# Moving the input and the first forward transform of a spectral layer ahead of a kernel's set-up

## The chip, the cores and the metric

The kernel runs on one core of one Trainium2 chip. The metric is the device time of one execution in microseconds (us); the median over runs is what counts. A core has five engines that run side by side, each through its own queue in order: PE (TensorE, matrix products), DVE (VectorE), ACT (ScalarE), POOL (GpSimd) and SP (SyncE, which here only issues DMA transfers). An instruction that waits holds up everything behind it on its engine.

## The reference

Four layers are interleaved on one sequence `x` of 2048 rows and 512 columns: A, B, A, B, each as `x = x + layer(layernorm(x))`, in 32-bit floats.

```python
def A(x, w_r, w_i):                       # spectral layer
    X = rfft2(x, axes=(-2, -1))           # 2048 x 512 -> 2048 x 257 complex
    return irfft2(X * (w_r + 1j * w_i), s=(2048, 512), axes=(-2, -1))

def B(u, A_re, A_im, B_re, B_im, C_re, C_im, log_dt, Dskip):   # state space layer
    dt = exp(log_dt)[:, None]                                  # 512 channels, 128 states
    P = exp((dt * (A_re + 1j*A_im))[:, :, None] * arange(2048))
    K = einsum("dn,dnl,dn->dl", C, P, dt * B).real             # 512 kernels of 2048 taps
    return causal_convolution(u, K) + u * Dskip                # by FFTs of length 4096
```

The layer norm takes mean and variance over the 512 columns. Layer B's kernel `K` depends on the weights alone, is computed once, and serves both B layers.

## The kernel before

All transforms are matrix products with tables of cosines and sines. `x` lies in SBUF as 128 partitions by 16 slices by 512; a *slice* is one of the 16 values of the index `s2`.

The first part of the program, up to about 370 us, does three things that don't depend on each other.

**The set-up of B's kernel (`setup_k`, L969).** From the weights (`kN`, `kLn`, loaded to `an` and `ld`) DVE and ACT work out the factors of the exponents: phases in turns (`th`, and three more quarters of a tile `F`) and logarithms. `parts` (L957) splits each factor in three bfloat16 parts: a cast on ACT, a subtraction on DVE, a store to DRAM (`spe`, `spt`), three times over. `load_k` (L1026) reads them back, 16 rows at a time, in another layout. All loads of `load_k` wait for all stores.

**The units of B's kernel.** 32 units in eight batches of four. A batch begins with six exponentials (`exp_k`, L1043 to L1059: two products on PE, one ACT exponential of 128x1024 each, at L1057). A unit (`unit_k`, L1061) then rounds its phase (ACT L1071, DVE L1073 and L1074), takes a cosine and a sine (ACT L1076 and L1077), multiplies (DVE L1084 and L1085, POOL L1088 and L1089), makes 64 small products on PE (L1101) and copies the result (DVE L1112). ACT has to load another function table between exponentials, sines and square roots (ACT_TABLE_LOAD in the profile). Pieces called `turn_k` (copies at L1150) and `spectra_k` (copies at L823) carry finished kernels on.

**Layer A, first pass.** `loads` (L467) brings the weights `kN` and then `x` in eight transfers of two slices. `moments` (L488) takes mean and variance of a slice on DVE; `spread` (L497) turns four slices' variances into 1/sqrt. `forward_a` (L533) is the forward transform of one slice: the norm (here on DVE, L518), sum and difference of the halves on POOL (L543, L544), two more sums with reversed operands on DVE (L549, L550) and a copy of two columns on ACT (L551), four products on PE (L556, L559), a copy out of PSUM on ACT (L564). When all 16 are there, 16 pieces `first_a` (L652) do the transform over the slices, the product with the weights and the way back: `fold_d` on PE (L577), copies on ACT (L667, L668), products (L677 to L681), DVE L686 to L688 and L694, POOL L692, products (L703 to L711), a copy on ACT (L715). `inv_a` (L718) goes back to `x`.

The second part (layer B, A, B) starts when both are done.

**What sets the order.** The program is written out piece by piece by a planner (`Clock`, L197). It holds a set of Python generators, each with a rank; at each step it takes, of the pieces that its own estimate of times (`COST`, L40) says can start by about the same moment, the one with the lowest rank, and lets it emit its instructions up to the next `yield`. What a `yield` names are the engine, the buffers and the events waited for; a leading `+` says that the piece need not wait for what it has just emitted. So the order on every engine is fixed when the kernel is built. In `plan_k` the set-up has rank -99 (L1161); in `plan_a` the moments have -20 and the forwards `RANK[0] + RANK[1] * s2`, that is -4 and up (L1223, L1227).

Buffers come from rings: a table gives a name, a size and how many there are (`RINGW`: the temporaries `a`, `b`, `c`, `d` of a forward). The five buffers `G` for the tables of `first_a` lie in the space of `x` itself (`RINGX`), so their loads wait for the norms that read that part of `x`.

## Time and profile before

| what | value |
|---|---|
| median of 3 runs | 863.92 us (862.75 to 873.96) |
| the profiled execution | 864.92 us, of which the span from first to last instruction is 863.1 us |
| PE busy | 661.6 us, 77% of the span |
| DVE busy | 537.3 us, 62% |
| ACT busy | 406.4 us, 47% |
| POOL busy | 290.6 us, 34% |
| mean granted clock of PE | 0.934 |

Line numbers such as L1057 are those of the kernel before; the changed kernel has other numbers for the same lines. A row of the timeline gives the start and the duration in us, the engine, the line, the operation, the tile written, the tile read, their shape, and in square brackets the idle time ahead of it with what ended it. An answer by windows gives for each stretch the length and, for each engine, busy time and number of instructions, then the granted clock of PE, the share of the DMA engines and GB/s. DVE and POOL instructions overlap their neighbours by some 0.1 us, so what one costs in a row of them is the distance from start to start.

### The profile page before, as it was taken

The numbers are of one execution on the slowest core, as the hardware profiler recorded it, in microseconds if no ns is written. First come the engines' busy times: TensorE is split into PE (matmuls) and PEld (weight loads), VectorE is DVE, ScalarE is ACT, GpSimd is POOL, SyncE is SP. The second block draws the span as 40 slices with busy tenths as digits, with TensorE's granted clock in tenths as the row PEclk, the third lists the DMA queues.
The fourth block names the chain that finished last, engine by engine and source line by source line (L and its number), as shares of the span: only waits on it lengthen the run. The fifth ranks groups of instructions, "written<-read, shape, count | busy, mean of one in ns | idle before, by whom it ended". The sixth has DMA issues, their size and how long they took to land. (4 is left out here: it accounts for less than half of the span.)

```text
span 863.1 us, 23197 instructions
## 1 busy us (share of the span) xinstructions
PE 661.6 (77%) x9828; PEld 418.7 (49%) x9828; DVE 537.3 (62%) x1054; ACT 406.4 (47%) x742; POOL 290.6 (34%) x259
## 2 busy tenths in 40 slices
PE   0048677978999799797885876889877999488876
PEld 0036454646657444356332642767665544234555
DVE  6988866557848685963441643686876666267512
ACT  1447677487778857744243132175441234323120
POOL 0037745336526431500422314174443000067310
PEclk9999789899999999999898888899997999889988
DMA  9134005332524754469969971901641145957857
GB/s 330 46 124 125 13 13 160 107 116 90 178 91 149 259 163 135 155 213 242 249 156 262 272 275 42 221 2 37 225 170 43 26 123 142 276 148 188 233 128 211
DMA packets 86630, 132.48 MB, mean 153 GB/s; under 512 B 5660, under 2 KB 58144, under 8 KB 85888
## 3 DMA queue, kind: packets, MB, share of 16 engines
q1 hardware_dynamic: 54400, 101.65, 39.6%
q10 hardware_dynamic: 32128, 29.37, 11.8%
q8 instruction: 77, 1.26, 0.6%
q14 instruction: 25, 0.20, 0.1%
HBM read 70.31 MB, written 27.13 MB: 113 GB/s over the span
## 5 line engine op out<-in xcount | busy, mean ns | idle before, releaser
L880 POOL TENSOR_TENSOR wk<-wk 128x512 f32<-128x512 f32 x64 | 80.1, 1275 | 246.8 <-DVE wk L874 162.2
L874 DVE TENSOR_TENSOR wk<-ps,Y 128x512 f32<-128x512 f32 x128 | 79.1, 683 | 77.1 <-issue 28.2
L1088 POOL TENSOR_TENSOR Y<-wk,Y 128x1024 f32<-128x1024 f32 x32 | 76.4, 2386 | 111.7 <-issue 63.1
L915 PE MATMUL ps<-wk,cRbT 64*128 64x256 f32 x512 | 74.1, 438 | 21.7 <-DMA wk<-Ya 14.8
L556 PE MATMUL ps<-cRa,wk 128*128 128x256 f32 x128 | 36.0, 406 | 57.1 <-POOL wk L543 57.1
L915 PEld LDWEIGHTS ps<-wk,cRbT 64*128 64x128 f32 x512 | 61.3, 219 | 35.0 <-issue 15.7
L891 PE MATMUL ps<-wk,Y 32*32 32x256 f32 x2048 | 58.9, 405 | 19.3 <-POOL wk L880 10.7
L921 DVE TENSOR_TENSOR x<-x,ps 128x256 f32<-128x256 f32 x64 | 24.8, 408 | 72.6 <-PE ps L915 72.5
L770 PE MATMUL ps<-wk,cRb 128*32 128x256 f32 x1024 | 61.3, 381 | 6.4 <-DVE wk L518 4.0
L772 ACT COPY wk<-ps 128x512 f32<-128x512 f32 x64 | 37.1, 587 | 57.6 <-PE ps L770 35.6
L1073 DVE SCALAR_TENSOR_TENSOR wk<-wk,ps 128x1024 f32<-128x1024 f32 x32 | 38.9, 1214 | 40.2 <-ACT wk L1071 40.2
L732 PE MATMUL ps<-cDaT,apart 128*32 128x256 f32 x256 | 60.3, 385 | 1.3 <-DVE x L747 1.1
L543 POOL TENSOR_TENSOR wk<-wk 128x256 f32<-128x256 f32 x32 | 25.6, 800 | 90.1 <-DVE wk L518 55.5
L556 PEld LDWEIGHTS ps<-cRa,wk 128*128 128x128 f32 x128 | 23.4, 202 | 61.1 <-POOL wk L543 57.9
L770 PEld LDWEIGHTS ps<-wk,cRb 128*32 128x32 f32 x1024 | 37.8, 110 | 31.1 <-DVE wk L518 5.0
L1041 PE MATMUL ps<-wk,Y 96*128 96x512 bf16 x128 | 41.2, 401 | 13.0 <-DVE Y L1084 6.0
L1101 PE MATMUL ps<-Y 128*32 128x64 f32 x2048 | 40.0, 236 | 14.2 <-POOL Y L1089 7.4
L891 PEld LDWEIGHTS ps<-wk,Y 32*32 32x32 f32 x2048 | 27.1, 105 | 48.9 <-POOL wk L880 23.2
L899 ACT COPY Ya<-ps 128x256 f32<-128x256 f32 x64 | 19.4, 385 | 63.9 <-PE ps L891 46.1
L1057 ACT ACTIVATE Y<-ps 128x1024 f32<-128x1024 f32 x48 | 46.5, 1034 | 6.1 <-PE ps L1041 6.0
L518 DVE TENSOR_SCALAR wk<-x,mv,rs 128x256 f32<-128x256 f32 (+1 forms) x80 | 35.3, 481 | 21.6 <-PE ps L770 15.5
L1101 PEld LDWEIGHTS ps<-Y 128*32 128x32 f32 x2048 | 34.4, 120 | 29.1 <-issue 15.2
(190 smaller groups left out, 1542.9 us busy)
## 6 DMA issues: line engine op xcount, KB each, us to landing
Y<-khat SPq DMA_DIRECT2D x24, 512.0 KB, 7.9
yk<-wk ACTq DMA_DIRECT2D x32, 256.0 KB, 2.6
wk<-Y SPq DMA_DIRECT2D x16, 512.0 KB, 4.6
wk<-Ya SPq DMA_DIRECT2D x16, 512.0 KB, 4.6
Y<-in_W_dram SPq DMA_DIRECT2D x12, 515.0 KB, 4.0
x<-in_cPa_dram SPq DMA_DIRECT2D x16, 384.0 KB, 3.2
Y<-in_cGa_dram SPq DMA_DIRECT2D x12, 384.0 KB
x<-in_W_dram SPq DMA_DIRECT2D x16, 258.0 KB, 3.5
```

Source lines behind the costliest of these rows:

```text
L556: nc.tensor.matmul(p[:, 0:256], pq[:, i, :], self.Ra[:, i:i + 2].rearrange("p a m -> p (a m)"), start=i == 0, stop=i == 1)
L732: nc.tensor.matmul(p[32 * i:32 * i + 32, o:o + 256], self.folded(r, i)[:, b, s2].rearrange("p g m -> p (g m)"), self.DaT[:, b, :], start=b ...
L770: self.nc.tensor.matmul(p[o:o + 32, 256 * h:256 * h + 256], self.Rb[:, 2 * h + j, 32 * a:32 * a + 32], xn[s], start=True, stop=True)
L874: nc.vector.tensor_tensor(t[c][:, j], x, kh[:, j, ::-1, :] if c else kh[:, j], op=OP.mult)
L880: nc.gpsimd.tensor_tensor(Z[:, :, c], t[0][:, :, c], t[1][:, :, c], op=op)
L891: nc.tensor.matmul(v[j][h][i:i + 32], gi[o:o + 32, j, 4 + 2 * s + c, :], Z[o:o + 32, j, c, :], start=c == 0, stop=c == 1)
L915: nc.tensor.matmul(q[s], self.RbT[o, i, :], y[o, i, :], start=i == 0, stop=i == 3)
L1041: self.nc.tensor.matmul(p, f[:, c:c + 128], self.oh[:k, o:o + 512], start=True, stop=True)
L1057: nc.scalar.activation(m[:, :, 1024:] if i == 2 else m[:, i, :1024], p.rearrange("p (i m) -> p i m", i=2) if i == 2 else p, AF.Exp)
L1073: nc.vector.scalar_tensor_tensor(s, c, MAGIC, p, op0=OP.subtract, op1=OP.subtract)
L1088: nc.gpsimd.tensor_tensor(E[:, 0, :1024], c, m[:, :1024], op=OP.mult)
L1101: nc.tensor.matmul(pk[32 * j:32 * j + 32, 64 * e:64 * e + 64], E1[:, r, i, :], E2[:, r, i], start=r == 0, stop=r == 1)
```

## The change

Five edits, all in the first part of the program, but for small changes of shape in the second forward pass.

- `loads`: `x`'s first transfer, then layer A's table `cRa`, then `x`'s second transfer stand ahead of the weights `kN`; the remaining transfers of `x` follow.
- Ranks: the moments have -120, the forwards -116 and up, and of the set-up one chain has -130 and the others -110 and -105. So the forwards are emitted among the set-up.
- `NORMS[0]` is True: the norms of the first forwards are one ACT instruction (`Identity` with scale and bias), with one more small DVE instruction for each four slices (the bias).
- In the first pass (`r == 0`) the two reversed sums on DVE and the small copy on ACT are gone. POOL makes the difference in two instructions, the second with both operands reversed, and PE makes the four sums by adding two products in PSUM; one of them uses the negated table. A forward has then six products in place of four. A row of the table `cDa` is placed elsewhere to match.
- `setup_k` is split: `setup_b` (the complex product, logarithms, arctangent), `setup_a` (phases, `th`), and four `setup_f` that cast and store a quarter of `F` each. They share DVE and ACT instruction by instruction. The casts have three buffers for `hi` and `hj` and write quarters: 15 casts and 15 stores in place of 6 and 6.

```diff
-NORMS = False, False, True, False
+NORMS = True, False, True, False
...
     def loads(self):
         src = self.io["A_x"].rearrange("b (p s) d -> p (b s) d", p=128)
-        self.load_n()
-        self.mark("kN")
-        yield self.emitted("kN")
         for q in range(8):
-            if q == 0:
-                self.load_ra()
             self.nc.sync.dma_start(self.x[:, 2 * q:2 * q + 2, :], src[:, 2 * q:2 * q + 2, :])
-            for i, f in ((0, "load_h"), (5, "load_da"), (7, "load_rb")):
+            self.mark("in", q)
+            yield self.emitted(("in", q))
+            for i, f in ((0, "load_ra"), (1, "load_n"), (5, "load_da"), (6, "load_h"), (7, "load_rb")):
                 if i == q:
                     getattr(self, f)()
-            self.mark("in", q)
-            yield self.emitted(("in", q))
+            if q == 1:
+                self.mark("kN")
+                yield self.emitted("kN")
...
     def forward_a(self, r, s2, st):
-        yield "DVE a", self.after((id(st), s2 // 4)), ...
+        yield ("DVE a" if r else "ACT a"), self.after((id(st), s2 // 4)), ...
         xn = self.norm(s2, st)
         yield "POOL c d"
...
-        nc.gpsimd.tensor_tensor(uv.rearrange("p a b -> p (a b)"), lo, hi, op=OP.subtract)
+        if r:
+            nc.gpsimd.tensor_tensor(uv, lo, hi, op=OP.subtract)
+        else:
+            nc.gpsimd.tensor_tensor(uv[:, 0:129], lo[:, 0:129], hi[:, 0:129], op=OP.subtract)
+            nc.gpsimd.tensor_tensor(uv[:, 130:258], lo[:, 255:127:-1], hi[:, 255:127:-1], op=OP.subtract)
...
-        for b in range(2):
-            nc.tensor.matmul(p[:, 256 + 128 * b:384 + 128 * b], F[:, b, :], self.Ra[:, 0], start=True, stop=True)
+        if r:
+            for b in range(2):
+                nc.tensor.matmul(p[:, 256 + 128 * b:384 + 128 * b], F[:, b], R, start=True, stop=True)
+        else:
+            for i, o in enumerate((p[:, 256:384], p[:, 384:512])):
+                nc.tensor.matmul(o, uv[:, i:i + 128], R, start=True, stop=False)
+                nc.tensor.matmul(o, uv[:, 129 + i:257 + i], R if i else nR, start=False, stop=True)
...
-    def parts(self, a, shape, tag, out):
+    def parts(self, a, j, out):
         for p in range(3):
-            yield "ACT " + tag
-            hi = self.w(tag, shape).bitcast(BF)[:, :int(np.prod(shape[1:])) * 2]
-            nc.scalar.copy(hi, a)
-            if p < 2:
-                nc.vector.tensor_tensor(a, a, hi, op=OP.subtract)
-            nc.sync.dma_start(out(p), hi)
+            yield "ACT"
+            nc.scalar.copy(j[p], a)
+            nc.sync.dma_start(out(p), j[p])
+            self.mark("factors")
+            if p < 2:
+                yield "DVE"
+                nc.vector.tensor_tensor(a, a, j[p], op=OP.subtract)
...
+    def setup_f(self, a, r):
+        yield "ACT", self.after(("F", a), 1)
+        yield from self.parts(self.F[:, a, r], [h[:, a, r] for h in self.hi], ...)
...
-        yield -99, self.setup_k()
+        yield -130, self.setup_b()
+        yield -110, self.setup_a()
+        for a in range(2):
+            for r in range(2):
+                yield -105, self.setup_f(a, r)
...
-            yield -20, moments(s2)
+            yield -120, moments(s2)
...
-            yield RANK[0] + RANK[1] * s2, self.forward_a(0, s2, st)
+            yield -116 + s2, self.forward_a(0, s2, st)
```

Three places show what this does to the order. First DVE at the very start. `Y` holds the set-up's temporaries, `x` the input, `mv`, `rs`, `nb` the moments. Before:

```order
L1193 MEMSET quarter 128x1
L981 TENSOR_TENSOR Y<-Y 128x512 x2
L982 TENSOR_SCALAR Y<-Y 128x512
L953 TENSOR_SCALAR Y<-Y 128x512
L954 TENSOR_SCALAR Y<-Y 128x512
L955 SCALAR_TENSOR_TENSOR Y<-Y 128x512
```

Now, behind the moments of the first three slices:

```order
L491 BN_STATS st<-x 128x6
L492 BN_AGGR mv<-st 128x2
L501 RECIPROCAL rs<-rs 128x4
L504 SCALAR_TENSOR_TENSOR nb<-mv,rs 128x4
L1021 TENSOR_TENSOR Y<-Y 128x1024
L1023 TENSOR_TENSOR Y<-Y 128x1024
L1025 TENSOR_TENSOR Y<-Y 128x512
L1026 TENSOR_TENSOR Y<-Y 128x512
```

Four slices' moments and their 1/sqrt stand ahead of the set-up, which now begins with its other chain.

Second, ACT around the first batch of exponentials (L1057 before, L1102 now; `Ya` takes the forwards' copies, L564 before). Before:

```order
L551 COPY wk<-wk 128x2
L1057 ACT_TABLE_LOAD
L1057 ACTIVATE Y<-ps 128x1024
L551 COPY wk<-wk 128x2
L564 COPY Ya<-ps 128x128x4
L1057 ACTIVATE Y<-ps 128x1024
L564 COPY Ya<-ps 128x128x4
L551 COPY wk<-wk 128x2
L1057 ACTIVATE Y<-ps 128x2x512
L1057 ACTIVATE Y<-ps 128x1024
```

Now (`apart` takes the result of a `first_a`, L676 and L677 are its first copies, L971 is the set-up's last cast):

```order
L676 COPY wk<-ps 128x64
L677 COPY wk<-ps 128x448
L971 CAST Y<-Y 128x512
L724 COPY apart<-ps 128x64x8 x2
L1102 ACT_TABLE_LOAD
L1102 ACTIVATE Y<-ps 128x1024 x2
L1102 ACTIVATE Y<-ps 128x2x512
L1102 ACTIVATE Y<-ps 128x1024 x2
L1102 ACTIVATE Y<-ps 128x2x512
L1116 ACTIVATE wk<-ps,magic 128x1024 x2
```

The exponentials had 13 of the 16 forwards beside and behind them; now they have none, and two `first_a` are done and two more begun ahead of them.

Third, DVE at the end of the set-up (L965 before and L976 now are the subtractions between casts). Before:

```order
L965 TENSOR_TENSOR Y<-Y 128x2048
L503 RECIPROCAL rs<-rs 128x4
L493 BN_STATS st<-x 128x6
L494 BN_AGGR mv<-st 128x2
L493 BN_STATS st<-x 128x6
L494 BN_AGGR mv<-st 128x2
L493 BN_STATS st<-x 128x6
L494 BN_AGGR mv<-st 128x2
L518 TENSOR_SCALAR wk<-x,mv,rs 128x512 x2
```

Now:

```order
L1066 SCALAR_TENSOR_TENSOR Y<-Y 128x512
L1068 TENSOR_TENSOR Y<-Y 128x512
L976 TENSOR_TENSOR Y<-Y 128x512 x7
L695 TENSOR_TENSOR x<-ps,x 128x514
L696 TENSOR_TENSOR x<-ps,x 128x257
L697 TENSOR_TENSOR x<-ps,x 128x257
L976 TENSOR_TENSOR Y<-Y 128x512
L703 TENSOR_TENSOR x<-x 128x257
L695 TENSOR_TENSOR x<-ps,x 128x514
```

The moments and norms that followed the set-up are gone from there, and the set-up's last two subtractions stand behind the first products of `first_a` (L695 to L697).

Further down the first part's order on ACT differs in how many pieces of `first_a` and `turn_k` lie between two batches of exponentials. From the eighth batch on, ACT has the same instructions in the same order as before, to the end of the program, but for the small copy of the second forward pass.

More of the change, by code (lines that the diff above doesn't have):

```diff
@@ L535, in forward_a @@
         nc = self.nc
-        yield "DVE a", self.after((id(st), s2 // 4)), self.emitted(("grouped", 0, 1), 8 * r)
+        yield ("DVE a" if r else "ACT a"), self.after((id(st), s2 // 4)), self.emitted(("grouped", 0, 1), 8 * r)
         xn = self.norm(s2, st)
@@ new lines, in setup_a @@
+        self.turns_of(F[:, 1, 0], th, 32, k)
+        v.scalar_tensor_tensor(F[:, 1, 0], th, -0.5, F[:, 1, 0], op0=OP.mult, op1=OP.add)
+        self.mark("th")
+        yield "ACT hj hj hj"
+        hj = [self.w("hj", [128, 256]).bitcast(BF) for p in range(3)]
+        yield from self.parts(th, hj, lambda p: self.spt[p])
+    def setup_f(self, a, r):
+        yield "ACT", self.after(("F", a), 1)
+        yield from self.parts(self.F[:, a, r], [h[:, a, r] for h in self.hi], lambda p: self.spe[p, a, :, 512 * r:512 * r + 512])
@@ L987, in setup_k, with setup_b @@
+    def setup_b(self):
+        nc = self.nc
+        v = nc.vector
+        yield "DVE", self.after("kN")
+        an, F = self.an, self.F
+        four = [128, 4, 128]
+        an4 = an.rearrange("p r (c n) -> p r c n", c=4)
         ta, tb, w, u = (self.w(t, [128, 2, 512]) for t in ("W", "W", "U", "U"))
+        g, k2 = (self.w("k", [128, 512]) for _ in range(2))
         two = [128, 2, 512]
         v.tensor_tensor(ta, an[:, 4:6], an[:, 2:3].to_broadcast(two), op=OP.mult)
+        yield "+DVE"
@@ L990, in setup_k @@
         v.tensor_tensor(tb, an[:, 4:6], an[:, 3:4].to_broadcast(two), op=OP.mult)
+        yield "+DVE"
         v.tensor_tensor(w[:, 0], ta[:, 0], tb[:, 1], op=OP.subtract)
         v.tensor_tensor(w[:, 1], ta[:, 1], tb[:, 0], op=OP.add)
+        yield "ACT"
         nc.scalar.activation(u, w, AF.Abs)
-        g, k2 = (self.w("k", [128, 512]) for _ in range(2))
-        ln = an[:, 0:2]
+        ln = an[:, 2:4]
+        yield "DVE"
         v.scalar_tensor_tensor(ln[:, 0], u[:, 0], 1e-37, u[:, 1], op0=OP.max, op1=OP.max)
-        v.reciprocal(g, ln[:, 0])
+        for h in range(2):
+            yield "+DVE"
+            o = slice(256 * h, 256 * h + 256)
+            v.reciprocal(g[:, o], ln[:, 0, o])
@@ L1006, in setup_k @@
         v.tensor_tensor(k2, k2, u[:, 0], op=OP.add)
+        for h in range(2):
+            yield "+DVE"
+            o = slice(256 * h, 256 * h + 256)
+            v.reciprocal(k2[:, o], k2[:, o])
+        yield "+DVE"
         v.tensor_tensor(tb[:, 0], w[:, 1], g, op=OP.mult)
-        v.reciprocal(k2, k2)
         v.tensor_tensor(tb[:, 0], tb[:, 0], k2, op=OP.mult)
+        yield "ACT"
         nc.scalar.activation(tb[:, 0], tb[:, 0], AF.Arctan)
+        yield "+DVE"
         v.scalar_tensor_tensor(ln[:, 0], ln[:, 1], 0.5, ln[:, 0], op0=OP.mult, op1=OP.add)
-        v.tensor_tensor(F[:, 1, 1].rearrange("p (c n) -> p c n", c=4), an4[:, 0],
+        v.tensor_tensor(F[:, 1, 1].rearrange("p (c n) -> p c n", c=4), ln[:, 0].rearrange("p (c n) -> p c n", c=4),
@@ L1020, in setup_k @@
         v.tensor_tensor(f, f, tb[:, 0], op=OP.add)
-        yield "DVE"
-        yield from self.parts(th, [128, 256], "hj", lambda p: self.spt[p])
-        yield from self.parts(F.rearrange("p a r m -> p (a r m)"), [128, 1024], "hi", lambda p: self.spe[p].rearrange("a d m -> d a m"))
-        self.mark("factors")
+        self.mark("F", 1)
     def load_k(self, b):
-        yield "SP sq st", self.after("factors")
+        yield "SP sq st", self.after("factors", 15)
         sq, self.st[b] = self.w("sq", [96, 512]), self.w("st", [48, 512], BF)
```

72 lines of the change are left out of this document (43 added, 29 removed).

## The prediction

> **What bounds the kernel now.** The chain that ended last reaches back to 639 us only, so I begin with the busy time by windows, in the first 80 us.
>
> ```profile
> 0.00:20.00 20.00, 0.00 (x0) 0.00 (x0) 13.39 (x20) 3.05 (x5) 0.20 (x4) 1.00 0.91 324
> 20.00:40.00 20.00, 0.00 (x0) 0.00 (x0) 17.57 (x31) 9.93 (x11) 0.00 (x0) 1.00 0.19 68
> 40.00:60.00 20.00, 4.25 (x14) 3.59 (x15) 17.31 (x36) 7.87 (x10) 4.47 (x6) 1.00 0.27 97
> 60.00:80.00 20.00, 19.16 (x103) 14.43 (x103) 15.32 (x31) 15.42 (x30) 16.43 (x22) 1.00 0.63 182
> ```
>
> DVE has the set-up almost alone; PE and POOL do nothing for 55 us, then everybody is busy. The timeline gives the set-up's beginning, its last subtraction, its last cast, the read that waits for the last store, and the first exponentials' table load; the last row is from the tile `spe`:
>
> ```profile
> 5.32 1.29 DVE L981 TENSOR_TENSOR Y<-Y 128x512 f32<-128x512 f32 x2 [4.37 <-DMA Y<-in_kN_dram]
> 49.47 2.29 DVE L965 TENSOR_TENSOR Y<-Y 128x2048 f32<-128x2048 f32 x1 [0.77 <-ACT Y L963]
> 52.31 1.90 ACT L963 CAST Y<-Y 128x2048 bf16<-128x2048 f32 x1 [2.68 <-DMA spe<-Y]
> 57.03 0.93 SPq L1032 DMA_DIRECT2D Y<-spe  x1
> 63.10 1.28 ACT L1057 ACT_TABLE_LOAD   x1
> DMA to landing us min/median/max: 2.9/2.9/2.9
> ```
>
> From the end of the last cast (54.2) to the table load are 8.9 us: a store that lands after 2.9, a read, two products, and ACT copies of forwards that stand ahead. Each of the eight batches begins with this load. They stand at the edges of these windows (the eighth at 322.77):
>
> ```profile
> 63.10:104.52 41.42, 31.68 (x268) 23.15 (x267) 34.15 (x53) 28.90 (x47) 30.94 (x31) 0.91 0.28 82
> 104.52:131.71 27.19, 20.99 (x326) 13.81 (x324) 19.34 (x30) 22.66 (x27) 14.48 (x9) 0.83 0.05 12
> 131.71:178.30 46.59, 39.24 (x501) 27.32 (x502) 30.29 (x48) 28.49 (x38) 20.38 (x15) 0.93 0.47 149
> 178.30:207.97 29.67, 22.25 (x315) 14.40 (x317) 20.51 (x29) 23.80 (x28) 15.49 (x10) 0.94 0.26 81
> 207.97:244.52 36.55, 33.50 (x479) 23.88 (x468) 26.53 (x42) 26.80 (x35) 16.77 (x13) 1.00 0.50 155
> 244.52:279.70 35.18, 33.59 (x445) 22.84 (x444) 23.88 (x40) 27.81 (x36) 16.87 (x13) 0.95 0.37 115
> 279.70:322.77 43.07, 35.95 (x572) 17.63 (x571) 32.59 (x57) 29.98 (x37) 17.80 (x11) 0.96 0.62 208
> ```
>
> No engine is full. The short batches are near ACT's work (22.7 of 27.2, 23.8 of 29.7), the long ones near PE's (33.5 of 36.6). So a batch costs its own ACT time and something for each piece of layer A beside it. From the eighth load on the instructions stand in the same order on all engines before and after. The whole change is therefore two numbers: how much later the first table load stands, and how much shorter the way from the first load to the eighth is.
>
> **The way from the first load to the eighth.** ACT's work in the first part, by line:
>
> ```profile
> L1057 ACT ACTIVATE Y<-ps 128x1024 f32<-128x1024 f32 x48 | 46.5, 1034 | 6.1 <-PE ps L1041 6.0
> L1076 ACT ACTIVATE wk<-wk,quarter 128x1024 f32<-128x1024 f32 x32 | 36.7, 1147 | 14.8 <-DVE wk L1074 14.0 <-ACT wk L1150 0.6
> L1071 ACT ACTIVATE wk<-ps,magic 128x1024 f32<-128x1024 f32 x32 | 35.7, 1127 | 15.2 <-PE ps L1041 11.0 <-POOL Y L1089 2.9 <-ACT wk L1150 1.3
> L1077 ACT ACTIVATE ps<-wk 128x1024 f32<-128x1024 f32 x32 | 32.3, 1011 | 0.0
> L1150 ACT COPY wk<-ps 128x512 f32<-128x512 f32 x24 | 14.1, 589 | 8.7 <-DMA khat<-wk 3.1 <-PE ps L1145 2.8 <-DMA yk<-wk 1.5
> ```
>
> A batch alone is 6 x 1.03 + 4 x (1.15 + 1.13 + 1.01) + 2 table loads of 1.28 = 21.9 us. By the order, windows two to six hold 15 pieces of `first_a` (I count its first and second half as a half each) and 18 copies of `turn_k` and `spectra_k`, which I price at 0.59 each (L1150). These windows last 175.2 us in sum, so a `first_a` costs (175.2 - 5 x 21.9 - 18 x 0.59) / 15 = 3.7 us. The first window holds half a `first_a` and 13 forwards: (41.4 - 21.9 - 1.8) / 13 = 1.36 us for a forward. That is about what POOL takes for one (from start to start 1.46, below).
>
> After the change the same windows hold no forward, 12.5 instead of 15.5 `first_a`, and the same copies; the seventh is unchanged. Saved by these prices: 13 x 1.36 + 3 x 3.7 = 28.7 us.
>
> The windows aren't straight in their pieces, though: the one with four `first_a` (46.6) is 6.4 above this line, those with two are 1 to 2 below it (27.2 against 29.3). The change also spreads the pieces: 3, 2, 1.5, 1.5, 1.5 and 3 to a window. Priced by their nearest windows (27.2 for two, 29.7 with copies, 35.2 for the last, 31.5 halfway for the first) the six last 27.2 + 28.5 + 30.5 + 28.5 + 35 + 31.5 = 181 in place of 216.6: 35 us. I take **31**, nearer to the line, since one window makes the difference and I can't tell its excess from its clock of 0.93. The lower end: if `first_a` only fills time in which ACT idles, 17.7 remain; the upper is 35.
>
> **How much later the first load stands.** The rows I step with: moments, a two-input sum, an immediate scaling and a reciprocal of 512 columns on DVE; norms on ACT; PE's four products of a forward; POOL's first sum of two forwards in a row, between which lies the second.
>
> ```profile
> 43.22 0.66 DVE L493 BATCH_NORM_STATS2 st<-x 128x6 f32<-128x512 f32 x1
> 44.02 0.66 DVE L493 BATCH_NORM_STATS2 st<-x 128x6 f32<-128x512 f32 x1
> 13.17 0.68 DVE L992 TENSOR_TENSOR Y<-Y 128x512 f32<-128x512 f32 x1
> 22.16 0.43 DVE L1001 TENSOR_SCALAR Y<-Y 128x512 f32<-128x512 f32 x1
> 15.70 3.35 DVE L997 RECIPROCAL Y<-Y 128x512 f32<-128x512 f32 x1
> 551.66 1.50 ACT L516 ACTIVATE wk<-x,nb,rs 128x512 f32<-128x512 f32 x2
> 63.50 1.03 PE L556 MATMUL ps<-cRa,wk 128*128 128x256 f32 x4
> 64.36 0.61 PE L559 MATMUL ps<-cRa,wk 128*128 128x128 f32 x4
> 64.81 1.03 PE L556 MATMUL ps<-cRa,wk 128*128 128x256 f32 x4
> 577.43 0.77 POOL L543 TENSOR_TENSOR wk<-wk 128x256 f32<-128x256 f32 x1
> 578.89 0.77 POOL L543 TENSOR_TENSOR wk<-wk 128x256 f32<-128x256 f32 x1
> ```
>
> A forward on PE goes from 1.31 to 1.76 us (0.86 + 2 x 0.45). On POOL the halved difference costs 0.45 an instruction (an estimate: half of the 0.73 from start to start, and 0.1 for what is fixed), 1.6 a forward; no row has POOL read backwards. DVE reads backwards in L549 and pays nothing for it, so I take nothing; the bounds are 0 and double price (0.9 x 16 = 14 us, of which POOL's idle time covers about half).
>
> What decides is how DVE and POOL get along:
>
> ```profile
> 56.34 0.72 POOL L543 TENSOR_TENSOR wk<-wk 128x256 f32<-128x256 f32 x1
> 56.42 0.80 DVE L549 TENSOR_TENSOR wk<-wk 128x127 f32<-128x127 f32 x1 [1.21 <-POOL wk L544]
> 58.33 0.28 DVE L549 TENSOR_TENSOR wk<-wk 128x127 f32<-128x127 f32 x1
> 64.58 0.54 DVE L518 TENSOR_SCALAR wk<-x,mv,rs 128x512 f32<-128x512 f32 x1
> 64.66 1.04 POOL L543 TENSOR_TENSOR wk<-wk 128x256 f32<-128x256 f32 x1 [0.52 <-DVE wk L550]
> ```
>
> A sum of 0.28 us takes 0.80 when POOL is inside one: it ends 0.16 after POOL does. The other way round POOL takes 1.04 in place of 0.72. So they run in turn, each saving some 0.1 us of overlap. The Trainium skill has this as a rule (SBUF — State Buffer, section "SBUF: two separate sides"): DVE instructions with two SBUF inputs or in a two-port mode and GpSimd instructions take one port pair as an exclusive lock. It speaks against this change, which puts 16 forwards of POOL beside a set-up of just such DVE instructions; the rows agree. Without it the sum is that of the first rival.
>
> Now the steps, with times in the new kernel.
>
> To 17 us: before, the set-up began at 5.3 with the first half of `kN`; now `x`'s first transfer lands about there, the moments of four slices take 4 x 0.8, and after the square root the first norm starts near 9. `kN` lands near 10, behind 1 MB more. The product of `setup_b`, 2 x 1.15 + 2 x 0.61, and the first forwards take turns until 15; two moments to 17.
>
> To 33: Abs waits on ACT behind the copies of two forwards, whose products PE makes slowly after a long rest, until 19.6. Then DVE does 0.7 + 3.35 + 1.2 + 2 x 0.8 + 0.6 + 0.45 = 7.9, to 27.5, and ACT three table loads, Ln, Exp and the second group's square root: 3 x 1.28 + 1.06 + 0.63 + 0.2 = 5.7. The fifth norm starts at **33**. POOL has been idle for 14 us: the order on ACT puts the set-up's logarithm ahead of it.
>
> To 58: up to the last square root ACT has 6 norms, 4 copies, the arctangent and two table loads, 4.5 + 2 + 0.6 + 2.6 = 9.7, and waits some 4 for POOL and PE: 47, with five forwards done on POOL. DVE stands still from 43 on, as its queue waits for this square root. Then five forwards and the set-up's 12 phase instructions go in turn: 5 x 1.6 + 4 x 0.65 + 8 x 0.5 = 14.6 less 0.1 at each of some 25 turns and less what POOL had ahead, about 11: **58**.
>
> To 73: the last norm ends at 59, and the casts stand behind it on ACT. DVE sets the pace: ten subtractions of 0.61, three sums of 0.7, the products of two `first_a` ahead of the last two subtractions, 2 x 1.5, and some 2.5 of waiting for POOL and for those products. The last cast ends at **73**.
>
> Then a store, a read and the exponentials' products, without copies of forwards between: 5.5 us in place of 8.9. The first load comes at 78.5 instead of 63.1: **15.4 us later**. The ends: 7 (the first rival) and 28 (the third).
>
> The moved DMAs cost nothing: 15 stores of 128 KB at issue costs of 0.4 us hide behind the casts, as they no longer wait for a buffer (2.68 above); the loads of `G` ahead of them on SP wait for norms that are done before the casts.
>
> The Trainium skill gives a change of function set 1.28 us plus a drain of 1.38 (ScalarE: Activation LUTs, section "What ACT_TABLE_LOAD costs"). With the drain the three loads ahead of the fifth norm would add 4 us, and the sum would be some 4 worse. The trace shows no drain behind the load:
>
> ```profile
> 21.42 1.28 ACT L1002 ACT_TABLE_LOAD   x1
> 22.71 1.06 ACT L1002 ACTIVATE Y<-Y 128x1024 f32<-128x1024 f32 x1
> ```
>
> Sum: 864.9 + 15.4 - 31 = 849.3 for the profiled execution. The median lies 1.0 below it before, so I predict **848.3**.
>
> **The rivals.** *The turns cost little.* If DVE's waits fall into time it would idle anyway, the forwards go at PE's 1.76 us from 33 on: the last norm ends near 51, the last cast near 65, the load 7 us late. With 31 saved the median is 840, with 35 it is 836. For it: DVE is idle some 3 us at two places in my steps. Against it: DVE was 17.6 of 20 us busy.
>
> *`first_a` filled idle time.* Only 17.7 us are saved, the load is 15.4 late: 861.6. For it: ACT idles 4.5 of 27.2 us in the second window. Against it: PE is 92% busy in the fifth.
>
> *The start eats more than the rest gives.* One mechanism: the casts stand behind the last norm on ACT, the norm behind POOL, POOL behind DVE. If DVE's and POOL's turns leave no overlap and POOL pays double for reading backwards, POOL's last 12 forwards need 3 us each, the last norm is at 69, the load 26 to 28 late. Against 17.7 saved that is 872 to 874; against 31 it decides from a first load later than 63.1 + 31 = 94, with 17.7 already from 81. Here both have to come together.
>
> That the change doesn't do what it says can be left out: the order shows the forwards ahead of the first exponential.
>
> **How the numbers follow.** The forecast with a spread of 6 us to both sides has 0.53, the first rival 0.22, the second 0.17, the third 0.08. A measurement of this kernel tells 2%, 17.3 us, from no change: below 846.6 or above 881.2. Faster by more: nearly all of the first rival (0.20) and over a third of the forecast (0.20), 0.40. Slower by more: the third with a third of its chance, 0.03. Within: the rest, 0.57. The range from 836 to 863 takes in the first two rivals and leaves out the third and the edges.
>
> **What would show it.** In the changed profile: the first norm near 9; POOL idle from about 19 to 33; DVE sums of the set-up near 0.3 to 0.5 us longer than 0.61 to 0.69 between 48 and 58; the last norm on ACT near 58, the last cast near 73, the first exponentials' load near 78.5; from there to the eighth load 229 us in place of 259.7, 31 to 33 of it in the first batch; and from there to the end 540 us as before. The prediction is wrong if the eighth load moves by another amount than the end does, if the first batch is not shorter by 8 or more, or if the first load stands before 70 or after 90.

## The result, and the profile after

The changed kernel takes **842.64 us** (median of 4, 840.87 to 843.16), the kernel before beside it 867.2: a ratio of 0.973, 95% interval 0.969 to 0.977. It is faster. The forecast was 848.3, the range 836 to 863. The profiled execution is 843.16 us, its span 841.3.

Below, the eighth table load splits an execution in two. The program behind it is the same in all kernels here unless I say otherwise. Ratios go by undisturbed executions (here without the 873.96 us of the kernel before), and the profile of the new operations in the old order is of a disturbed one (875.8 us, median 869.1), so of it only the part ahead of the eighth load is read.

First the answer by windows for the changed kernel: its first 80 us in four pieces, the seven windows from one exponentials' table load to the next, then the three stretches up to the first load, to the eighth, and to the end. The columns are the stretch, its length, then busy time and number of instructions of PE, of PE's weight loads, of DVE, ACT and POOL, and at the end the granted clock, the share of the DMA engines and GB/s.

```profile
0.00:20.00 20.00, 9.60 (x47) 8.67 (x48) 11.95 (x25) 10.52 (x15) 9.20 (x16) 1.00 0.93 333
20.00:40.00 20.00, 6.31 (x24) 5.40 (x24) 19.48 (x34) 12.59 (x15) 6.78 (x10) 0.57 0.44 138
40.00:60.00 20.00, 17.04 (x102) 15.34 (x102) 11.51 (x19) 13.96 (x21) 15.65 (x25) 0.91 0.30 81
60.00:80.00 20.00, 17.87 (x124) 15.55 (x125) 14.12 (x24) 12.16 (x27) 3.69 (x6) 1.00 0.42 133
80.90:109.10 28.20, 23.14 (x240) 16.13 (x238) 17.49 (x26) 23.97 (x30) 10.64 (x8) 0.88 0.31 92
109.10:134.26 25.16, 20.26 (x348) 13.82 (x348) 20.37 (x32) 22.68 (x26) 13.45 (x11) 1.00 0.20 64
134.26:162.74 28.48, 22.76 (x341) 13.48 (x340) 23.82 (x34) 23.78 (x28) 15.11 (x12) 0.94 0.51 158
162.74:195.16 32.42, 26.89 (x401) 17.56 (x401) 20.22 (x31) 24.96 (x31) 13.26 (x10) 0.84 0.24 70
195.16:222.07 26.91, 20.86 (x292) 12.04 (x295) 21.31 (x32) 23.71 (x28) 14.00 (x11) 0.97 0.56 172
222.07:258.25 36.18, 35.22 (x504) 24.30 (x497) 22.83 (x38) 27.76 (x35) 14.98 (x12) 0.93 0.34 106
258.25:304.28 46.03, 39.23 (x573) 18.73 (x571) 31.99 (x57) 30.25 (x36) 15.10 (x11) 0.89 0.58 194
...
0.00:80.90 80.90, 51.71 (x296) 45.61 (x296) 57.64 (x101) 49.81 (x78) 35.93 (x55) 0.87 0.52 171
80.90:304.28 223.38, 188.35 (x2684) 116.06 (x2682) 158.02 (x247) 177.11 (x211) 96.55 (x69) 0.92 0.40 127
304.28:841.28 537.00, 437.89 (x6914) 268.49 (x6914) 298.35 (x671) 195.84 (x466) 148.56 (x151) 0.93 0.59 168
```

The same three stretches of the kernel before:

```profile
0.00:63.10 63.10, 7.17 (x29) 5.48 (x30) 51.08 (x90) 22.21 (x30) 7.01 (x13) 1.00 0.46 164
63.10:322.77 259.67, 217.20 (x2887) 143.02 (x2885) 187.29 (x294) 188.43 (x247) 132.75 (x96) 0.93 0.39 122
322.77:863.10 540.33, 437.20 (x6914) 270.19 (x6914) 298.89 (x671) 195.77 (x466) 150.86 (x151) 0.93 0.59 167
```

| stretch | before | after | difference | forecast |
|---|---|---|---|---|
| start to first load | 63.10 | 80.90 | +17.80 | +15.4 |
| first to eighth load | 259.67 | 223.38 | -36.29 | -31 |
| eighth load to the end | 540.33 | 537.00 | -3.33 | 0 |

PE does 51.7 us of its work before the first load in place of 7.2, POOL 35.9 in place of 7.0. The shorter way comes from the first window (28.20 in place of 41.42), the third (28.48 for 46.59) and the fifth (26.91 for 36.55). The seventh, with the same order as before, is 3 us longer.

Then the start. These are rows of the timeline of the changed kernel, first ACT, then DVE, then POOL:

```profile
8.73 1.52 ACT L514 ACTIVATE wk<-x,nb,rs 128x512 f32<-128x512 f32 x2 [0.44 <-DVE nb L504]
32.34 1.51 ACT L514 ACTIVATE wk<-x,nb,rs 128x512 f32<-128x512 f32 x2
58.47 0.82 ACT L514 ACTIVATE wk<-x,nb,rs 128x512 f32<-128x512 f32 x1 [1.13 <-POOL wk L546]
59.65 1.14 ACT L971 CAST Y<-Y 128x512 bf16<-128x512 f32 x2
72.08 0.62 ACT L971 CAST Y<-Y 128x512 bf16<-128x512 f32 x1 [2.06 <-DVE Y L976]
74.47 0.62 ACT L971 CAST Y<-Y 128x512 bf16<-128x512 f32 x1 [0.67 <-DVE Y L976]
80.30 0.59 ACT L724 COPY apart<-ps 128x512 f32<-128x512 f32 x1 [3.28 <-PE ps L720]
80.90 1.28 ACT L1102 ACT_TABLE_LOAD   x1
```

```profile
11.14 1.81 DVE L1021 TENSOR_TENSOR Y<-Y 128x1024 f32<-128x1024 f32 x1 [2.45 <-DMA Y<-in_kN_dram]
22.59 1.23 DVE L1037 TENSOR_TENSOR Y<-Y 128x1024 f32<-128x1024 f32 x1
47.73 0.18 DVE L501 RECIPROCAL rs<-rs 128x4 f32<-128x4 f32 x1 [5.74 <-ACT rs L499]
```

```profile
10.30 0.47 POOL L545 TENSOR_TENSOR wk<-wk 128x129 f32<-128x129 f32 x1
10.72 0.47 POOL L546 TENSOR_TENSOR wk<-wk 128x128 f32<-128x128 f32 x1
11.82 1.45 POOL L545 TENSOR_TENSOR wk<-wk 128x129 f32<-128x129 f32 x1
33.22 0.73 POOL L541 TENSOR_TENSOR wk<-wk 128x256 f32<-128x256 f32 x1 [14.61 <-ACT wk L514]
```

First norm at 8.7, fifth at 32.3 with POOL idle for 14.6 us ahead of it, last norm over at 59.3 (58.47 and 0.82); all fifteen casts (from 59.65, last one over at 75.1) stand behind that norm on ACT. The first load waits for the copy L724 of a `first_a` that the planner put ahead of it.

### The profile page after: what moved, and what is told of

Same layout as the page of the kernel before. It is cut to its first block, busy times and chain, and to the rows that moved or that the text cites. A ratio compares the mean times of both kernels' runs of the same rounds, so it can differ in the third digit from the quotient of the medians.

```text
span 841.3 us, 23370 instructions
## 1 busy us (share of the span) xinstructions
PE 677.9 (81%) x9892; PEld 430.2 (51%) x9892; DVE 514.0 (61%) x1019; ACT 422.8 (50%) x755; POOL 281.0 (33%) x275
## 5 line engine op out<-in xcount | busy, mean ns | idle before, releaser
L883 DVE TENSOR_TENSOR wk<-ps,Y 128x512 f32<-128x512 f32 x128 | 79.1, 682 | 72.6 <-issue 27.5
L1133 POOL TENSOR_TENSOR Y<-wk,Y 128x1024 f32<-128x1024 f32 x32 | 66.3, 2071 | 116.6 <-issue 64.3
L924 PE MATMUL ps<-wk,cRbT 64*128 64x256 f32 x512 | 70.3, 416 | 22.4 <-DMA wk<-Ya 14.0
L924 PEld LDWEIGHTS ps<-wk,cRbT 64*128 64x128 f32 x512 | 57.9, 205 | 34.9 <-issue 14.8
L559 PE MATMUL ps<-cRa,wk 128*128 128x256 f32 x128 | 38.4, 428 | 28.0 <-POOL wk L541 27.2
L900 PEld LDWEIGHTS ps<-wk,Y 32*32 32x32 f32 x2048 | 27.4, 107 | 47.7 <-POOL wk L889 23.6
L1102 ACT ACTIVATE Y<-ps 128x1024 f32<-128x1024 f32 x48 | 46.1, 1027 | 8.6 <-PE ps L1086 8.4
L1129 DVE TENSOR_TENSOR Y<-ps,Y 128x1024 f32<-128x1024 f32 x32 | 39.0, 1218 | 14.0 <-ACT ps L1122 13.7
L908 ACT COPY Y<-ps 128x256 f32<-128x256 f32 x64 | 19.6, 384 | 52.2 <-PE ps L900 52.2
```

The source lines that it names most:

```text
L883: nc.vector.tensor_tensor(t[c][:, j], x, kh[:, j, ::-1, :] if c else kh[:, j], op=OP.mult)
L900: nc.tensor.matmul(v[j][h][i:i + 32], gi[o:o + 32, j, 4 + 2 * s + c, :], Z[o:o + 32, j, c, :], start=c == 0, stop=c == 1)
L924: nc.tensor.matmul(q[s], self.RbT[o, i, :], y[o, i, :], start=i == 0, stop=i == 3)
L1102: nc.scalar.activation(m[:, :, 1024:] if i == 2 else m[:, i, :1024], p.rearrange("p (i m) -> p i m", i=2) if i == 2 else p, AF.Exp)
L1129: nc.vector.tensor_tensor(E[:, 1, :1024], p, m[:, :1024], op=OP.mult)
L1133: nc.gpsimd.tensor_tensor(E[:, 0, :1024], c, m[:, :1024], op=OP.mult)
```

## The experiments

I read the gain as one of **order**: thirteen forwards, and some of `first_a`, leave the batches, where each lengthens a batch, and are done beside the set-up, where PE and POOL stood idle. The rival: **the cheaper operations** pay (norms off DVE, reversed sums in PSUM, where PE's products land), wherever they stand. Two more questions are inside the first theory: what the turns of DVE and POOL cost, and what sets the first load.

### One half of the change at a time, the planner free

Four kernels. `e1_order_only` is the kernel before with the loads and the ranks of the changed one; its set-up stays in one piece:

```diff
-        yield -99, self.setup_k()
+        yield -100, self.setup_k()
...
-            yield -20, moments(s2)
+            yield -120, moments(s2)
...
-            yield RANK[0] + RANK[1] * s2, self.forward_a(0, s2, st)
+            yield -116 + s2, self.forward_a(0, s2, st)
```

> The kernel before with the new order alone (loads of x first, all sixteen forward sums ahead of the exponentials, the set-up in one piece ahead of them); the norms and the reversed sums stay on VectorE, the set-up is not cut in two. If the gain is one of order (forward sums taken out of the exponential batches and done while GpSimd and TensorE stand idle): the way from the first to the eighth table load falls to about 223 to 232 us as in the changed kernel, the first load comes at 85 to 95 us because VectorE has 15 to 20 us more to do before it, and the time is 850 to 860 us. If the gain is one of the cheaper operations (norms on ScalarE, sums in PSUM), the order alone gives nothing: 864 us or more.

`e4b_forwards_beside` is its opposite, the changed operations with forwards 3 to 15 beside the exponentials; the loads, the moments and the first three forwards stay where the change put them:

```diff
-        yield ("DVE a" if r else "ACT a"), self.after((id(st), s2 // 4)), ...
+        yield ("DVE a" if r else "ACT a"), self.after((id(st), s2 // 4)), ..., self.emitted("exp", 0 if r or s2 < 3 else 2)
```

> The changed kernel with all its cheaper operations, but forward sums 3 to 15 held back until the second exponential has been issued, so that they lie beside the exponentials as in the kernel before. By the theory of order: first load at 55 to 60 us, first window 40 to 47 us, way from the first to the eighth load 245 to 260 us, time 858 to 866 us. If the cheaper operations pay by themselves: 850 us or less.

Two more undo one operation in the changed kernel: `e2_norms_dve` (`NORMS[0]` False again) and `e3_sums_on_dve` (the sums L549 and L550 and the copy L551 of the kernel before are back, and the rings with them).

> The changed kernel with the norms of the first forward on VectorE again (16 operations of the kind that takes 0.4 to 0.6 us there). By the theory of order the way from the first to the eighth table load stays at 222 to 226 us and only the first load moves, 3 to 8 us later, for VectorE carries the set-up: 846 to 851 us. If the move of the norms is what pays, the time goes back to 858 us or more. If VectorE has room for them (it stood still from 42 to 47.7 us), the time stays within 2 us of the changed kernel's.

> The changed kernel with the reversed sums of the first forward on VectorE again (sum and difference as two VectorE operations and ScalarE's copy ahead of them, in place of the added products in PSUM). By the theory of order the way from the first to the eighth load stays within 4 us of 223, and the first load comes 5 to 15 us later by VectorE's extra 13 pairs: 848 to 858 us. If the sums in PSUM are what pays, 860 us or more.

Measured: 888.87, 875.68, 863.79 and 877.16 us; against the kernel before 1.030 (1.022 to 1.037), 1.015 (1.008 to 1.022), 1.001 (0.998 to 1.004), 1.016 (1.009 to 1.023). All four miss what the theory of order gave, and all to the slow side. By the letter of their expectations, `e1`, `e2` and `e3` even speak for the cheaper operations (864, 858 and 860 us or more). These rows of `e2_norms_dve` show a reason that has nothing to do with norms:

```profile
300.09 1.28 ACT L1102 ACT_TABLE_LOAD   x1 [0.63 <-ACT wk L1195]
312.54 1.28 ACT L499 ACT_TABLE_LOAD   x1
316.19 1.28 ACT L1102 ACT_TABLE_LOAD   x1 [0.51 <-ACT wk L832]
```

The last batch of exponentials is torn apart by a square root, so the exponentials' table is loaded nine times, not eight. The same happened in all four. A small edit at the start had shifted the planner's estimates, and it wrote another order from the seventh load (266.05 in `e2`) on. A kernel compared this way is two kernels apart, so I repeated all four with the order fixed.

### The same four with the order fixed

The planner takes the pieces in an order recorded from another kernel:

```diff
-            t, p = min((e for e in ready if e[0] <= now), key=lambda e: e[1][:2])
+            t, p = min(ready, key=place)
```

`place` is the number of a piece's next step in the record. `e2p` and `e3p` follow the changed kernel throughout, `e1p` follows it from the first exponential on, and `e4bp` follows the kernel before once the sixteen forwards are out. With that, engine by engine, they have from there on the order of the kernel they follow.

> The kernel before with the new order alone, as in the run of that kind before it, but from the first exponential on every instruction is emitted in the recorded order of the changed kernel, so that the planner cannot choose another second part. From the loads seen there: first load near 98.6 us, seventh near 281, eighth 46 us later at 327, and 537 to 540 us from there to the end as in the kernels before and changed: 865 to 869 us, no change against the kernel before. If the second part's order is not what made that run slower, it stays at 882 us or more.

> The changed kernel's operations in the kernel before's order: forward sums beside the exponentials, and from the sixteenth forward sum on every instruction in the recorded order of the kernel before. From the loads of the run that left the planner free: first load near 56.8 us, the way to the eighth load as before (255 to 260 us), 537 to 540 us to the end: 855 to 860 us, so the cheaper operations alone give 5 to 10 us. If the other second part was not what made that run slower, 870 us or more.

> The changed kernel in its own recorded order throughout, with the norms of the first forward on VectorE again. First load near 86 us (5 later than in the changed kernel), way to the eighth load 223 to 228 us, 537 us to the end: 847 to 852 us. If the norms on ScalarE are worth the 21 us that the run with a free planner lost, 860 us or more.

> The changed kernel in its own recorded order throughout, with the reversed sums of the first forward on VectorE again. First load 88 to 93 us, way to the eighth load 223 to 229 us, 537 us to the end: 852 to 860 us. If the sums in PSUM are worth the 34 us that the run with a free planner lost, 870 us or more.

| kernel | median us | against before (95%) | first load | first to eighth load | eighth load at |
|---|---|---|---|---|---|
| before | 863.9 to 867.2 | 1 | 63.10 | 259.67 | 322.77 |
| `e4bp`: new operations, old order | 869.10 | 1.005 (1.001 to 1.009) | 57.05 | 269.83 | 326.88 |
| `e1p`: old operations, new order | 876.75 | 1.014 (1.005 to 1.023) | 98.56 | 231.37 | 329.93 |
| after: both new | 842.64 | 0.973 (0.969 to 0.977) | 80.90 | 223.38 | 304.28 |
| `e2p`: norms on DVE again | 845.48 | 0.978 (0.972 to 0.985) | 82.60 | 220.86 | 303.46 |
| `e3p`: sums on DVE again | 863.21 | 0.996 (0.992 to 1.000) | 89.92 | 226.12 | 316.04 |

Fixing the order gave 12.1, 6.6, 18.3 and 14.0 us of the medians back (e1, e4b, e2, e3 against their fixed forms). So the other order was a cause, and in `e2` it was 18.3 of the 21.2 us to the changed kernel. What the torn batch costs by itself, apart from the rest of that order, wasn't measured. None of the four medians lies in its expected range: `e2p` comes out 1.5 us below it, `e3p` 3.2 above, `e1p` 7.8 above and `e4bp` 9.1 above, so the prices that I put on the halves were rough.

What follows. **Neither half pays alone.** The eighth load comes 4.1 us later with the operations alone, 7.2 us later with the order alone, 18.5 us earlier with both; the rival falls, and so does my first theory in its simple form. The rows say why. The windows of `e4bp`, its start and its first batch:

```profile
0.00:57.05 57.05, 7.64 (x36) 6.57 (x36) 46.28 (x89) 30.20 (x43) 7.67 (x13) 0.70 0.48 165
57.05:110.27 53.22, 38.53 (x323) 30.35 (x324) 13.78 (x18) 37.83 (x48) 29.68 (x45) 0.81 0.29 82
```

In the old order the new operations bring the first load forward by 6 us, but the first batch takes 53.2 us in place of 41.4: the norms are now on ACT beside the exponentials, and ACT is busy for 37.8 us in place of 28.9. Thirteen norms of 0.75 us are 9.8. (`e4b`, the same up to there but for the planner's freedom, agrees: first load at 56.75, first batch 55.9 us.) The same norms in the new order stand ahead of the exponentials. By these rows the old order with the cheaper sums but with the norms left on DVE might have kept the 6 us; that kernel wasn't run, so that the operations don't pay alone is shown only for all of them together.

The start of `e1p`, then its way:

```profile
0.00:98.56 98.56, 45.31 (x203) 36.20 (x204) 68.96 (x132) 35.57 (x65) 32.18 (x38) 0.81 0.39 137
98.56:329.93 231.37, 194.38 (x2716) 120.68 (x2712) 163.01 (x251) 178.67 (x214) 113.18 (x70) 0.91 0.39 124
```

In the new order the old operations save 28.3 us on the way and lose 35.5 at the start. DVE has 69.0 us of work before the first load in place of 57.6, but that sum alone isn't the reason: `e2p`, below, has 66.5 and its load at 82.60. So the order makes the saving (28 us with the old operations, 36 with all the change), and the operations make the start cheap enough for it: 17.8 us later, not 35.5.

**Of the operations, in the new order, the sums count and the norms don't.** Taking the norms back to DVE moves the first load by 1.7 us and the eighth by -0.8; DVE has 66.5 us of work before the first load in place of 57.6, and had the room. The medians differ by 2.8 us with overlapping intervals.

```profile
0.00:82.60 82.60, 50.33 (x296) 44.01 (x296) 66.49 (x113) 38.63 (x63) 37.19 (x55) 0.90 0.51 167
```

Taking the sums back moves the first load by 9.0 and the eighth by 11.8. These rows of ACT in `e3p` show where:

```profile
59.30 0.81 ACT L538 ACTIVATE wk<-x,nb,rs 128x512 f32<-128x512 f32 x1
...
62.24 0.19 ACT L574 COPY wk<-wk 128x1 f32<-128x1 f32 x1 [1.66 <-POOL wk L566]
62.33 0.81 ACT L538 ACTIVATE wk<-x,nb,rs 128x512 f32<-128x512 f32 x1
...
67.86 1.13 ACT L992 CAST Y<-Y 128x512 bf16<-128x512 f32 x2
```

The little copy of one column waits for POOL's difference, and the next norm stands behind it. Norms follow each other at 2.5 to 3.0 us (from 51.86 on; in the changed kernel at 1.5 to 2.7), and the first cast comes at 67.86, not 59.65. How much of this is the copy's wait, how much DVE's 32 sums and how much the rings that came back with them (two buffers of `c` and `d` in place of three) wasn't separated. The splitting of the set-up was not tried alone; if the parts add up, it is worth, together with the order that the planner chose for the start of `e1p`, the other 14.7 of the 25.65 us between `e1p` and the changed kernel at the eighth load.

### Is it the work side by side that pays?

`e4p_forwards_behind` is the changed kernel in its own recorded order, with forwards 3 to 15 held until the fifteen casts are out:

```diff
+        ..., self.emitted("factors", 0 if r or s2 < 3 else 15)
```

> The changed kernel in its own recorded order, but forward sums 3 to 15 held back until all fifteen casts of the set-up have been issued, still ahead of the exponentials. The run with the forward sums beside the exponentials had its first load at 57 us with the set-up alone on VectorE; thirteen forward sums of about 1.5 us of GpSimd follow, so the first load comes at 76 to 80 us, with the eighth 223 us behind. If doing the forward sums under the set-up gains little, because VectorE and GpSimd only take turns there: 838 to 845 us, as the changed kernel. If the work side by side is what pays: the thirteen forward sums come on top with their waits, first load at 88 us or more, 850 us or more.

Measured: 869.23 us, 1.002 (0.998 to 1.006); first load at 109.65, eighth 222.1 behind it. My number was 76 to 80, so this is a miss by 30 us, and the side-by-side theory is right: as the forwards stand in this kernel, it is worth 28.7 us at the first load. The rows of ACT:

```profile
57.55 0.62 ACT L995 CAST Y<-Y 128x512 bf16<-128x512 f32 x1 [0.24 <-DVE Y L1000]
58.07 0.81 ACT L538 ACTIVATE wk<-x,nb,rs 128x512 f32<-128x512 f32 x1
...
94.05 0.58 ACT L597 COPY Ya<-ps 128x512 f32<-128x512 f32 x1 [1.17 <-PE ps L592]
...
109.65 1.28 ACT L1126 ACT_TABLE_LOAD   x1
```

Without forwards beside it the set-up is done at 58.2, 17 us sooner than in the changed kernel. But then thirteen forwards take 36.5 us, 2.8 each in place of the 1.5 of POOL's own time that I had counted: norm, sums, products and copy run in a chain through four engines with two or three buffers. And the `first_a`, whose tables are loaded into the space of `x` behind the norms, add 15 us more. So the 28.7 is an upper figure: the order of norms and copies on ACT was written for another place, and PE's clock was at half for the first of these forwards (last section).

### What the turns cost, and what sets the first load

`e6_pool_tiny` keeps every instruction and the order (with one memset more on POOL at the start), but POOL's sums of the first forward work on 4 columns, so most of each sum is left out.

> The changed kernel in its own order, with GpSimd's sums of the first forward on 4 columns in place of 256, 129 and 128: most of the sums of the first forward are left out, and the output is not the reference's. This measures what GpSimd's time and the turns it takes with VectorE cost. If the turns are what holds the set-up back: first load at 68 to 74 us, the eighth 223 us behind, 830 to 836 us. If the set-up's own chain of ScalarE and VectorE holds it: first load at 78 us or later, 839 us or more.

Measured: 834.77 us, 0.963 (0.955 to 0.971); first load at 75.78. Between the two numbers, so neither theory as I put it: POOL's time and its turns with DVE cost 5.1 us of the start. POOL's work ahead of the first load fell from 35.9 to 15.2 us, and the load still came at 75.8. An instruction of 4 columns still takes 0.2 us or more, so 5.1 us is the price of the part that was left out.

`e5_casts_first` holds the products of the early `first_a` back until the casts are out:

```diff
-        yield "DVE t1a t2a"
+        yield ("DVE t1a t2a",) if r else ("DVE t1a t2a", self.emitted("factors", 15))
```

> The changed kernel, but the products of the first stages ahead of the exponentials wait until the set-up's fifteen casts have been issued, so that VectorE does its last two subtractions 7 us earlier. By the step of the prediction that puts the last cast behind those products: last cast near 70 us in place of 75, first load 3 to 6 us earlier, 837 to 841 us. If the transfer through device memory or the products themselves set the first load anyway: within 1 us of the changed kernel.

Measured: 840.31 us (833.4 to 844.6), 0.967 (0.960 to 0.974); first load at 75.89, 5.0 earlier. The expectation held for the load, though the last cast ends at 72.6, not 70. But most of the 5.0 us come from the load's place: the second copy of a `first_a`, which it waited for, now stands behind it, and the first copy starts at 75.28 in place of 76.43. What the load is for, the first exponential, moves by 3.3 us. Its row in the changed kernel, then in `e5`, where the products ahead of it wait for the read of the stored factors:

```profile
82.85 2.85 ACT L1102 ACTIVATE Y<-ps 128x1024 f32<-128x1024 f32 x3 [0.66 <-PE ps L1086]
```

```profile
79.53 1.94 ACT L1102 ACTIVATE Y<-ps 128x1024 f32<-128x1024 f32 x2 [2.36 <-PE ps L1086]
```

So the waits of 2.06 and 0.67 us ahead of the last casts cost something, but less than 5.0 us. In the whole time the step down from 842.6 is within what four executions spread.

`e10_no_standstill` starts from it and moves DVE's reciprocal of the fourth statistic (it waited 4.7 us there for ACT's square root) behind three steps of the phases.

> The kernel with the casts first, in its own recorded order with one thing moved: VectorE's reciprocal and shift of the fourth statistic stand behind three more steps of the phases, so that VectorE does not stand still for ScalarE's last square root (4.7 us there, from 42.5 to 47.2 us). About 3.5 us of work fit into that gap. If the standstill is on the path to the first exponential: first load at 71.5 to 73.5 us in place of 75.9, the eighth 222 us behind, 834 to 838 us. If the time comes back as turns with GpSimd, whose sums then meet the same VectorE steps: first load at 75 us or later, 839 to 842 us.

Measured: 839.70 us, 0.971 (0.965 to 0.976); first load at 78.67, 2.8 later than without the move. The first expectation is wrong, and the second one too in its reason. DVE's rows:

```profile
48.54 0.18 DVE L525 RECIPROCAL rs<-rs 128x4 f32<-128x4 f32 x1 [2.92 <-ACT rs L523]
...
53.60 0.83 DVE L1023 SCALAR_TENSOR_TENSOR Y<-Y 128x512 f32<-128x512 f32 x1
62.35 0.89 DVE L1000 TENSOR_TENSOR Y<-Y 128x512 f32<-128x512 f32 x1 [7.92 <-ACT Y L995]
```

DVE finishes its phases 2.5 us sooner and then waits 7.9 us for the first cast, which on ACT stands behind the last norm. The norms end later: the recorded order also put two copies that wait for PE ahead of the last norms on ACT, so this kernel changes two things, and what the move of the reciprocal is worth alone isn't shown. A column over the kernels that start in the changed kernel's order, the last two with the casts first, shows what is common to them:

| kernel | first cast on ACT | first load | between |
|---|---|---|---|
| after | 59.65 | 80.90 | 21.3 |
| `e6_pool_tiny` | 53.77 | 75.78 | 22.0 |
| `e2p`, norms on DVE | 59.66 | 82.60 | 22.9 |
| `e3p`, sums on DVE | 67.86 | 89.92 | 22.1 |
| `e5_casts_first` | 58.91 | 75.89 | 17.0 |
| `e10_no_standstill` | 61.70 | 78.67 | 17.0 |

The start of the changed kernel is set by the forwards' chain up to the last norm on ACT, and by a nearly fixed way of casts and `first_a` behind it: 21 to 23 us in the changed kernel's order, 17 with the casts first, where the load waits for one copy less (from the first cast to the first exponential it is 23.2 us in the changed kernel and 20.6 in `e5`). DVE's phases have slack there: DVE is through with those ahead of the casts at 57.7 and then waits 2.60 us for the first cast. In `e2p`, where the norms are on DVE, it is the other way round, and the first cast waits for the phases:

```profile
60.30 0.89 DVE L976 TENSOR_TENSOR Y<-Y 128x512 f32<-128x512 f32 x1 [2.60 <-ACT Y L971]
```

```profile
59.66 1.14 ACT L995 CAST Y<-Y 128x512 bf16<-128x512 f32 x2 [2.77 <-DVE Y L988]
```

So which of the two chains sets the first cast depends on where the norms are: on ACT it is the norms' own chain, on DVE the phases that the norms delay.

## Why the prediction was right

**The sum** was 849.3 for the profiled execution, the measurement is 843.16. The three terms missed by +2.4 (start), -5.3 (way) and -3.3 us (rest), 6.2 together; the first offsets a part of the others, which is luck.

**The start, +15.4, measured +17.8.** The steps held closely: first norm near 9 (8.73), fifth norm at 33 (32.34) with POOL idle 14 us (14.61), DVE's standstill from 43 to 47 (42.0 to 47.7), last norm over at 59 (59.29). The mis-sized term is the last one, "some 2.5 of waiting" and the last cast at 73: it came at 75.1, with 2.7 us of waiting at the last two casts alone, and in `e5`, without most of it, the last cast ends 2.5 us sooner and the first exponential starts 3.3 us sooner. The 5.5 us from the last cast to the load were 5.8, but not for the store and the read that I named: the load stands behind a copy of `first_a` that waited 3.28 us for PE, and the first exponential, behind the load, waits only 0.66 us more. The rows of the turns are as foretold: DVE's first product took 1.81 us beside POOL and the like of it (L1037) 1.23 alone, POOL's sums 1.45 in place of 0.47. That is the rule that the Trainium skill gives (SBUF — State Buffer, section "SBUF: two separate sides"), and the trace agrees. The fifth norm at 32.3, not 4 us later, also bears out that no drain stands behind a table load, where the Trainium skill has one (ScalarE: Activation LUTs, section "What ACT_TABLE_LOAD costs"). But the sentence "What decides is how DVE and POOL get along" was too strong: `e6` prices the greater part of POOL's time and the turns together at 5.1 us of the 17.8.

**The way, -31, measured -36.3.** I had two prices and leaned to the wrong one. The first six windows take 177.4 us; by the nearest windows they were to take 181, by the straight line 187.9. The term that was mis-sized is the excess of the window with four `first_a` over the line: it was real, and it means that the price of 3.7 us for a `first_a` was too high. The same arithmetic on the changed kernel gives 3.1 in windows two to six ((149.15 - 5 x 21.9 - 18 x 0.59) / 9.5) and 2.1 in the first ((28.2 - 21.9) / 3). The first batch was shorter than I said (28.2 against 31 to 33), and the seventh longer by 3.0 without any change in its order.

**The rest, 0, measured -3.3.** No change of order there, so no term. But one of the prediction's own signs of being wrong was that the eighth load moves by another amount than the end does: it moved by -18.5, the end by -21.8. So "The whole change is therefore two numbers" holds to some 3 us only: as the last section shows, the stretch behind the eighth load takes different times with one and the same order, and 3.3 us of the gain are not accounted for.

**The rivals.** The first (the turns cost little, load 7 us late, 840) gives a time that is nearer to the measured one than the forecast, but by another way: its load would stand at 70, and it stood at 80.9; even with POOL's work cut to 15.2 us it stood at 75.8. The second (`first_a` filled idle time, 861.6) falls by the 36 us. The third (the start eats the gain) did not come with the whole change. Its arithmetic, not its mechanism, is what `e1p` shows: old operations in the new order, the load at 98.56, beyond the 94 that I gave as the deciding point, and the kernel slower.

What the prediction didn't see is how much the two halves need each other. It priced the operations as costs of the start only, and nothing in it says that the order alone makes the kernel 1.4% slower.

## What to carry to other kernels

Work taken from the middle of a program into idle time at its start has two prices, what the middle saves and what the start cannot hide; make it cheap on the chain that bounds the start before it is moved, or the move can lose, as in `e1p`. To find what bounds a start, change one step at a time and look for the interval that stays the same: here 21 to 23 us from the first cast to the load, whatever was done to DVE or POOL. Where a planner writes the order, an experiment has to fix the order first: four edits of a few us were hidden here under 7 to 18 us of another order 200 us later.

## What the runs showed of the hardware beyond that

**Reading backwards on POOL costs nothing.** In the rows of POOL above, the reversed difference of 128 columns (L546) takes 0.47 us, the forward one of 129 columns (L545) 0.47.

**TensorE's clock fell to half early in the program in some executions, and cost little there.** In the window from 20 to 40 us the granted clock is 0.57. The starts of `e1_order_only` and of its fixed form had the same operations and first loads at 98.63 and 98.56; the row of the first stands here, that of the second above, with clocks of 0.97 and 0.81.

```profile
0.00:98.63 98.63, 45.97 (x203) 35.65 (x204) 69.89 (x132) 35.42 (x64) 32.14 (x38) 0.97 0.40 137
```

In `e4p`, where forwards are a chain, it shows in PE's products: the four products of a forward take twice as long while the clock is low (0.50 from 59.7 to 66.0 us, 1.00 from 72.2 to 74.0).

```profile
59.74 2.07 PE L583 MATMUL ps<-cRa,wk 128*128 128x256 f32 x4 [40.20 <-POOL wk L565]
...
72.17 1.03 PE L583 MATMUL ps<-cRa,wk 128*128 128x256 f32 x4
```

**The second part took from 533 to 547 us with one and the same order.** From the eighth load to the end: 540.3 (before), 537.0 (after), 538.7 (`e2p`), 546.7 (`e3p`), 543.4 (`e1p`), 540.7 (`e4p`), 533.7 (`e5`), 533.4 (`e6`), 535.3 (`e10`). Some 8 of the 9.7 us between the changed kernel and `e3p` arise in one stretch of layer B, from 455.6 to 471.2 us in the changed kernel and from 462.0 to 485.8 in `e3p`. From the waits in that stretch, in this order of the kernels, with total, number and longest:

```profile
PE ps L924 <- DMA wk<-Y: 1.4, 1, 1.4
```

```profile
PE ps L945 <- DMA wk<-Y: 9.4, 3, 6.5
```

PE waits 9.4 us for transfers that it waits 1.4 us for in the changed kernel. The DMA engines are nearly full in both stretches (busy for 1.00 and 0.93 of the time, 276 and 242 GB/s). Why the transfers land late when everything comes 12 us later is open, and so is whether the other executions of `e3p` have these 8 us too. It matters for the verdicts: of the 20.6 us between the medians of the changed kernel and `e3p`, the profiles put 11.8 ahead of the eighth load and the rest here.
